# Attention heads paired by kind, scores on two row halves of TensorE, w_in loaded pair by pair

## The chip, the cores and the metric

The kernel runs on one core of a Trainium2 chip. A core has five engines with instruction queues of their own: TensorE (PE in the profile, its weight loads PEld), VectorE (DVE), ScalarE (ACT), GpSimd (POOL) and SyncE (SP). Each works its queue off in order and waits for the others by semaphores. Transfers from and to HBM are issued from the queues of SyncE, ScalarE and GpSimd, and run on 16 DMA engines[...]. The metric is the time of the program on the device in microseconds; the median of three runs is given with the lowest and the highest.

## The reference

Attention over 4 batches, 8 heads, 768 positions of 64 elements, followed by a feed-forward layer with a parametric ReLU. Heads 0, 2 and 6 ("retrieval") see every earlier position. The other five ("streaming") see the first 4 positions (sinks) and the last 64.

```python
scores = q @ k.T / sqrt(64)
scores = where(mask, scores, -1e9)            # causal, or causal and (sink or within 64)
a = exp(scores - max); a = a / sum(a)
x = (a @ v)  ->  [3072 tokens, 8 heads * 64 = 512]
h = x @ w_in                                  # 512 x 2048
g = maximum(h, 0) + alpha * minimum(h, 0)     # alpha: one factor for each of 2048
out = g @ w_out                               # 2048 x 512
```

Inputs and output are fp32; the kernel multiplies in bf16 and sums in fp32.

## The kernel before, in words

**Segments.** Work is cut into 16 segments of one head pair each: segment n is batch n // 4, pair n % 4. A pair's two heads are hh = 0 and 1, and lie side by side on partitions 0 to 63 and 64 to 127 of q and of the attention result. `PAIRS` (line 98) is (0, 1), (2, 3), (6, 7), (4, 5): three pairs of a retrieval and a streaming head, one of two streaming heads.

**Items.** Each step has a short name, and the list `ORDER` (lines 14 to 70) says in what order the steps are recorded. Every engine gets its instructions in that order. No scheduler moves anything: what stands earlier in the list stands earlier in its engine's queue. The names, n for the segment, hh for the head, m for a part:

- `Lqn`, `Lkn`, `Lvn`: loads of q, k, v from SyncE's queue (`load_q` at line 196, `load_k` at 202, `load_rows` at 217). `Cq`, `Ck`, `Cv` cast to bf16, for batch 0 and part of batch 1 on GpSimd, later on VectorE.
- `Tq`, `Tk` transpose on TensorE (line 348) in batches 0 and 1, `tq`, `tk` copy the result to `qT` and `kT`. In batches 2 and 3 transposing DMAs (`Dq`, `Dk`) do it.
- `Sn.hh.m`: scores, `S_retr` (line 405) or `S_stream` (lines 438 and 444); `sn.hh.m`: exponential on ScalarE (lines 415, 463, 469); `mn.hh.m`: multiplication by the mask on VectorE. Batch 0 adds the mask on TensorE instead (lines 408 and 447). `kT` holds each head's k on its own 64 partitions with zeros on the others, so that a score matmul runs over all 128 rows and takes one head's q from the pair's.
- `An.hh`: A·V for the head (line 501), with a column of ones in `vb` for the sums; `an.hh`: reciprocal and multiplication on VectorE (lines 510 and 511).
- `Xn`, `xn`: the pair's result is transposed into `xT`, on TensorE (line 523) or by DMA.
- `Pt.f`: first layer of token block t, for 128 or 256 of the 2048 columns (P1, line 543); `pt.f`: ReLU of the negated on ScalarE (line 548); `gt.f`: combination on VectorE (line 555). In token block 0 the first six `P0.f` are cut into three parts by pair, so that they can start before the last pair is there.
- `Ot.s.u`: a quarter of the second layer for 128 tokens (P2, line 563); `ot.s`: copy on ScalarE and store (lines 569 and 573). The very last 128 tokens are computed in two column halves, `L0`, `L1` with `l0`, `l1` (line 579).
- `wi0` to `wi3`, `wo0` to `wo3`: loads of w_in and w_out from GpSimd's queue, which cast to bf16 on the way (lines 646 and 649). `gate` is one small GpSimd memset on a q buffer ahead of them. `La` loads alpha from ScalarE's queue, `Al` transposes it on TensorE (line 593).

**Tiles of queries.** Keys are cut into tiles of 128 rows. Which query tile starts where is held in `Tiles`: `FAR` (batches 0 and 1) steps by 124, `NEAR` (batches 2 and 3) by 112, since a streaming head's key tile also holds the four sinks. Both have seven query tiles; a retrieval head paired with a streaming head uses the same ones.

**Banks.** PSUM has eight banks. `take` picks, among those that an item may use, the bank given back longest ago; `give` hands it back. Scores use banks 0 and 1 (`SC`), the feed-forward layer 2 to 5 (`FF`), A·V and transpositions 6 and 7 (`MISC`); batch 0 and the ends have lists of their own (`SC2`, `LEAD`, `TAIL`).

Of the kernel before, what the change touches and what calls it, by code (L numbers as in the profile page):

```python
# [9 lines left out]
ALU = mybir.AluOpType  # L10
# [4 lines left out]
Lq0.0 sz0 id Lk0 Lq0.1 zero kz1 kz0 Lq1 nms vz3 kz2 nmr Ck0.0 warm Cq0.0 Tq0.0 Ck0.1 m13.0.2 qz0 Cq0.1 Lk1 sz2 Tk0.0  # L15
kz3 Lq2 Cq1 vz0 tk0.0 Tk0.1 tq0.0 S0.0.0 S0.0.2 Ck1.1 s0.0.0 Lv0 Tq0.1 S0.0.1 Ck1.0 Lk2 Tq1 s0.0.2 qz sz1 s0.0.1 tk0.1
gate tq0.1 Cq2 Cv0 Tk1 Ck2.0 tq1 Ck2.1 S0.1.1 vz1 tk1.0 s0.1.1 tk1.1 Lv1 so vo S0.1.0 s0.1.0 ro Lk3 Lq3 Tq2 S1.0.0 Cv1
s1.0.0 S1.0.2 idf A0.1 A0.0 s1.0.2 tq2 a0.1 S1.0.1 vz2 a0.0 wi0 S1.1.0 s1.0.1 Lv2 Tk2 A1.0 Ck3.1 S1.1.1 tk2.0 s1.1.0
S2.0.0 Cq3 s1.1.1 Ck3.0 s2.0.0 X0 a1.0 S2.0.1 kfz2 A1.1 Cv2 tk2.1 Tq3 a1.1 x0 Tk3 s2.0.1 tq3 tk3.0 S2.1.1 s2.1.1
S2.0.2 X1 S2.1.0 s2.0.2 A2.0 S3.0.1 s2.1.0 tk3.1 x1 S3.0.0 A2.1 s3.0.1 kfz0 La S3.1.0 a2.0 Lv3 P0.2.0 s3.0.0 wi1  # L20
S3.1.1 a2.1 X2 s3.1.1 s3.1.0 Cv3 A3.0 P0.0.0 x2 P0.2.1 a3.0 P0.0.1 Lk4 A3.1 P0.1.0 Al m4.0.2 P0.3.0 a3.1 Ck4.0 P0.1.1
P0.3.1 one X3 wi2 P0.5.0 x3 Ck4.1 P0.4.0 ms wi3 Lk5 P0.0.2 Ck5.0 P0.4.1 Lq4 P0.5.1 p0.0 P0.5.2 p0.5 P0.2.2 kfz1 P0.4.2
al Lv4 Cq4 p0.4 P0.3.2 g0.0 Ck5.1 g0.5 p0.3 p0.2 wo0 Lq5 Tk4 g0.4 g0.3 Tq4 tq4 P0.1.2 P0.6 P0.7 m14.0.2 p0.1 Tk5 P0.10
p0.7 g0.2 P1.0 tk4.0 Lk6 g0.1 Lq7 g0.7 p0.10 g0.10 Lq6 S4.0.1 wo2 p0.6 p1.0 S4.0.0 P0.11 g0.6 P0.9 mr g1.0 s4.0.1
S4.0.3 s4.0.0 S4.0.5 p0.11 s4.0.3 P0.12 wo1 p0.9 s4.0.5 g0.11 P0.14 tk4.1 nz0 p0.12 S4.0.4 g0.9 wo3 s4.0.4 S4.0.2
P0.13 Cq5 p0.14 tk5.0 S4.1.2 g0.12 Lk7 P1.4 P0.15 g0.14 m4.0.3 s4.0.2 tk5.1 S4.1.0 p0.13 s4.1.2 m4.0.4 Tq5 nr g0.13
m4.0.1 S4.1.1 P1.2 P0.8 p0.15 Lk8 Ck6.0 tq5 s4.1.0 s4.1.1 p1.4 S5.0.2 p0.8 s5.0.2 Lv5 Ck6.1 m4.0.0 m4.0.5 S5.0.0
s5.0.0 g0.15 Cv4 Cv5 g1.4 g0.8 A4.0 P1.12 Tk6 P1.8 p1.2 a4.0 S5.0.1 O0.1.0 Cq6 g1.2 p1.8 s5.0.1 m4.1.1 m5.0.0 Tq6
S5.0.4 tq6 s5.0.4 tk6.0 P1.6 p1.6 Lv6 Lq8 m4.1.0 S5.0.3 m4.1.2 g1.8 A4.1 O0.0.0 p1.12 S5.1.2 s5.0.3 O0.0.1 O0.0.2
tk6.1 s5.1.2 S5.0.5 S6.0.1 Cq7 Lq9 Ck7.1 g1.6 P1.10 s5.0.5 g1.12 a4.1 S5.1.0 m5.0.5 m5.0.1 p1.10 s5.1.0 Lv7 X4 Ck8 Tq7  # L30
m5.1.0 s6.0.1 O0.1.1 S5.1.1 Lk10 S6.0.4 m5.0.4 s6.0.4 O0.1.2 tq7 kfz3 nz1 Ck7.0 s5.1.1 g1.10 m5.0.3 O0.2.0 x4 S6.1.0
m5.1.1 Tk7 s6.1.0 A5.0 m5.1.2 m6.0.1 S6.0.2 tk7.0 tk7.1 O0.0.3 s6.0.2 m6.1.0 S7.0.0 S7.0.2 O0.1.3 s7.0.0 s7.0.2 S6.0.3
Cv6 Cq8 A5.1 O0.3.0 S6.1.1 o0.0 m6.0.4 m7.0.0 a5.1 P1.14 s6.0.3 m6.0.3 Dq8 Dk8.0 m7.0.2 S6.1.2 Cq9 s6.1.1 a5.0 p1.14
S6.0.0 s6.1.2 s6.0.0 O0.3.1 O0.3.2 S6.0.5 S7.0.1 m6.1.1 s6.0.5 X5 O0.2.1 m6.0.0 m6.1.2 g1.14 Lk9 m6.0.5 Dk8.1 S7.1.2
s7.0.1 S7.1.1 x5 s7.1.2 A6.1 O0.3.3 m7.0.1 m7.1.2 o0.3 S7.1.0 a6.1 s7.1.0 s7.1.1 Cv7 ns A6.0 O0.2.2 S8.0.0 m7.1.0
S8.0.4 Lq10 s8.0.0 O0.2.3 a6.0 O1.0.0 m7.1.1 A7.0 o0.1 S8.0.1 A7.1 Ck9 s8.0.4 S8.0.2 a7.0 s8.0.1 o0.2 Dq9 Dk9.0 Lv8
O1.0.1 S8.0.5 a7.1 Ck10 X6 s8.0.2 Dk9.1 Lq12 s8.0.5 S8.0.3 X7 x6 O1.0.2 S8.1.1 x7 s8.1.1 P2.0 O1.0.3 p2.0 S8.1.0
s8.1.0 P2.4 s8.0.3 p2.4 Cq10 S9.0.0 g2.0 P2.8 Dk10.1 near g2.4 o1.0 p2.8 P2.7 S9.0.1 m8.0.4 s9.0.1 m8.1.1 P2.5 m12.0.2
s9.0.0 P2.2 m8.0.0 Dq10 S8.1.2 p2.5 g2.8 Cv8 S9.0.2 s9.0.2 Lk12 s8.1.2 p2.7 O1.1.0 g2.5 O1.1.1 Dk10.0 g2.7 S9.0.4
m8.1.0 p2.2 g2.2 m8.1.2 P2.1 P2.13 S9.0.5 p2.1 s9.0.4 P2.9 p2.9 S10.1.0 g2.1 P2.6 m9.0.1 s9.0.5 p2.13 p2.6 Cq12 Lk11  # L40
Lq11 O1.1.2 s10.1.0 g2.9 m9.0.0 P2.3 S9.1.0 g2.13 p2.3 m8.0.5 P2.11 s9.1.0 g2.6 m8.0.3 A8.1 p2.11 m8.0.1 g2.11 A8.0
S10.0.5 P2.12 Lv9 g2.3 S9.1.1 s10.0.5 m9.0.4 Ck11 S10.1.2 P3.4 s10.1.2 S10.0.1 O1.1.3 P2.10 p3.4 a8.1 s10.0.1 s9.1.1
g3.4 S10.1.1 o1.1 s10.1.1 P3.10 Cq11 a8.0 S9.0.3 p2.12 P3.2 Lv10 S10.0.0 m9.1.0 p2.10 p3.10 Lq14 s9.0.3 g2.12 g2.10
g3.10 s10.0.0 P3.14 S9.1.2 Ck12 Cv9 s9.1.2 P2.15 S10.0.4 Dk11.1 p2.15 Dq11 O2.1.0 m9.1.1 m9.1.2 g2.15 m10.1.1 A9.1
m9.0.5 S10.0.3 O2.1.1 P2.14 s10.0.3 m9.0.3 p3.2 A9.0 g3.2 S11.1.2 p2.14 Dk11.0 m10.1.2 g2.14 O2.0.0 s10.0.4 p3.14 P3.6
m10.0.1 s11.1.2 g3.14 Dq12 S10.0.2 m10.0.5 S11.0.0 P3.0 s11.0.0 S11.0.1 Cq14 p3.0 s10.0.2 O2.0.1 a9.1 s11.0.1 m10.0.4
m10.1.0 Lv11 O2.0.2 Cv10 A10.1 O2.1.2 S11.1.0 S11.0.2 O2.0.3 Dk12.0 p3.6 s11.0.2 g3.0 a9.0 O2.1.3 Dk12.1 m11.0.1
S11.1.1 m10.0.0 m11.0.0 Lv12 Lk13 s11.1.0 m10.0.3 o2.1 o2.0 Cv11 A10.0 S12.0.5 s11.1.1 m11.0.2 X9 O2.2.0 m11.1.2 a10.1
S12.1.0 O2.3.0 s12.1.0 P3.8 Lk14 g3.6 a10.0 p3.8 A11.0 O2.2.1 m11.1.0 Lq13 O2.2.2 m11.1.1 S12.0.0 s12.0.5 A11.1
S12.0.3 g3.8 Ck13 X8 s12.0.3 P3.12 s12.0.0 S12.1.1 O2.2.3 m12.1.0 S12.0.4 Ck14 O3.0.0 s12.0.4 Dk13.0 s12.1.1 m12.0.0  # L50
S12.0.2 Cq13 m12.1.1 a11.0 s12.0.2 O3.0.1 O2.3.1 O2.3.2 S12.0.1 O3.0.2 p3.12 a11.1 Cv12 X10 m6.0.2 o2.2 Dq13 X11
m12.0.4 x11 O2.3.3 P4.5 s12.0.1 Dk13.1 Lq15 S13.0.0 s13.0.0 S12.1.2 g3.12 o2.3 m13.0.0 s12.1.2 O3.0.3 p4.5 Dk14.1 Dq14
S13.1.2 o3.0 P4.1 m12.0.5 g4.5 Cq15 S13.0.1 p4.1 P4.6 g4.1 P4.7 s13.1.2 S13.1.0 m12.0.3 m13.1.2 m12.0.1 p4.7 P4.0
s13.0.1 P4.10 p4.6 Lk15 A12.0 p4.0 g4.7 S13.0.3 Dk14.0 Lv13 s13.1.0 P4.4 S13.0.2 g4.0 m13.1.0 m12.1.2 p4.10 A12.1 P4.3
g4.10 s13.0.2 s13.0.3 g4.6 Ck15 Lv14 p4.4 g4.4 P4.8 p4.3 S13.1.1 S13.0.4 P4.2 g4.3 s13.1.1 a12.0 p4.8 s13.0.4 p4.2
P4.11 S14.1.0 g4.8 m13.0.1 g4.2 s14.1.0 m5.0.2 m13.0.4 p4.11 P4.15 S13.0.5 p4.15 g4.11 m13.1.1 S14.0.5 Dq15 Cv13
O3.1.0 s14.0.5 P4.12 s13.0.5 S14.0.1 S14.1.1 Cv14 m14.1.0 p4.12 g4.15 a12.1 Dk15.1 P4.14 s14.0.1 A13.1 Dk15.0 S14.0.3
g4.12 m13.0.3 P4.9 s14.1.1 S14.0.4 O3.1.1 m10.0.2 p4.14 s14.0.3 m13.0.5 s14.0.4 S15.1.0 S15.0.2 O3.1.2 s15.1.0 S14.0.0
P5.2 m14.1.1 Lv15 s14.0.0 g4.14 s15.0.2 a13.1 S14.1.2 X12 O3.1.3 A13.0 S15.0.0 o3.1 m14.0.1 P4.13 P5.10 p4.9 m14.0.4
g4.9 p5.2 m15.1.0 m14.0.5 s15.0.0 S14.0.2 s14.1.2 g5.2 S15.0.1 P5.0 P5.6 m14.1.2 p4.13 p5.10 s15.0.1 p5.0 m14.0.0  # L60
S15.1.2 g4.13 g5.10 O4.0.0 g5.0 A14.1 s15.1.2 O4.2.0 m15.0.1 S15.1.1 s14.0.2 O4.2.1 m15.0.2 m14.0.3 a14.1 p5.6 Cv15
m15.1.2 g5.6 O4.0.1 a13.0 A14.0 P5.8 P5.12 s15.1.1 m15.0.0 a14.0 A15.0 m15.1.1 O4.0.2 A15.1 a15.0 p5.8 O4.2.2 O4.0.3
a15.1 X15 g5.8 X14 O4.1.0 O4.1.1 O4.2.3 p5.12 O4.1.2 g5.12 O4.1.3 P5.4 X13 x15 P7.0 o4.1 O4.3.0 o4.0 p5.4 O4.3.1 P6.8
O4.3.2 P5.14 p6.8 g5.4 O4.3.3 P6.6 P6.12 p6.12 g6.12 O5.0.0 o4.2 O5.0.1 P7.6 p5.14 P6.13 g5.14 o4.3 P6.3 g6.8 p6.3
P7.2 g6.3 p7.0 O5.0.2 O5.1.0 p7.2 g7.0 P6.14 g7.2 p6.6 p6.13 g6.13 P6.7 P6.5 p6.5 O5.1.1 g6.6 P6.10 p6.14 P6.0 g6.14
g6.5 P6.2 O5.1.2 p6.7 p6.2 O5.1.3 g6.7 P6.1 O5.0.3 p6.10 g6.10 p7.6 P7.10 g7.6 P6.4 o5.0 o5.1 g6.2 P6.11 p6.0 P7.14
P6.9 p6.4 g6.0 p6.1 g6.4 p7.10 g7.10 P7.4 p7.4 O7.0.0 g6.1 P6.15 g7.4 P7.8 p6.9 p6.15 g6.9 p6.11 O6.2.0 g6.11 P7.12
O6.2.1 O6.1.0 g6.15 O6.0.0 O6.0.1 O6.2.2 O6.0.2 O6.2.3 p7.8 O7.0.1 O6.1.1 g7.8 o6.2 O6.1.2 O6.0.3 O6.3.0 m9.0.2 O6.1.3
O6.3.1 O6.3.2 m8.0.2 o6.0 p7.12 o6.1 g7.12 p7.14 g7.14 O7.0.2 O6.3.3 o6.3 O7.0.3 o7.0 L1 L0 l1 l0
""".split()  # L70


@with_exitstack
def kernel(
    ctx: ExitStack,
    tc: tile.TileContext,
    q: bass.AP,
    k: bass.AP,
    v: bass.AP,
    is_retrieval: bass.AP,  # L80
    n_sink: bass.AP,
# [10 lines left out]
    n_tok = B * S  # L92
    scale = 1.0 / (D ** 0.5)
    fp32 = DT.float32
    bf16 = DT.bfloat16

    RETR = [1, 0, 1, 0, 0, 0, 1, 0]
    PAIRS = [(0, 1), (2, 3), (6, 7), (4, 5)]
    NSINK = 4
    NT = 7  # L100
    SLOT = 256
    LAY = 8
    XD = (0, 1, 2)
    CROSS = 8
# [16 lines left out]
    def tiles(n):  # L121
        return NEAR if n >= LAY else FAR

# [232 lines left out]
    def put_k(key, n, hh, done=True):  # L356
# [6 lines left out]
        if done:  # L363
            give(held.pop(key))
# [426 lines left out]
```

## Time and profile before

| | |
|---|---|
| Median of 3 runs | 237.03 us (236.91 to 238.66) |
| Profiled execution, in all | 237.75 us |
| Its span | 236.0 us |
| TensorE busy | 226.6 us, 96% of the span |
| VectorE busy | 160.2 us, 68% |
| ScalarE busy | 137.1 us, 58% |
| GpSimd busy | 45.2 us, 19% |
| Matmuls recorded | 1997 (the program has 2026) |
| Read from HBM, written | 27.55 MB, 6.29 MB |

Times in the profile count from the start of the span. A row of a group names line, engine and operation, out and in tensors, and their shape; then its count, busy time and mean duration; then the idle time of the engine before it, with what ended most of it. A matmul's record lasts from its start to the end of its results, so the records of successive matmuls overlap, and the distance between starts is what one costs. The chain of waits is followed back from the last instruction, at each step to what released it, and merges like pieces. A few matmul records are missing. The granted TensorE clock was 1.00 throughout the profile.

### The profile page before, as it was taken

Reading aid. Unit: us, or ns where it says so; the run is one execution under the profiler, and the core shown is the slowest. Engines: PE = TensorE matmul, PEld = TensorE weight load, DVE = VectorE, ACT = ScalarE, POOL = GpSimd, SP = SyncE. Lnnn points to the kernel's source line nnn. Section 1 sums busy time; section 2 is a strip of 40 time slices with the busy share of each in tenths; the row PEclk is TensorE's granted clock in tenths of the full one; section 3 lists DMA queues with packets and bytes.
Section 4 is the critical chain, followed back from the end, with each engine's and each line's share of the span. In section 5 each row is a group of like instructions: output and inputs, shape, how many; then the busy total and the mean of one; then the engine's idle time right before and its main releaser. Section 6 shows DMA issues by size and latency. Waiting matters only on the chain.

```text
span 236.0 us, 5222 instructions
## 1 busy us (share of the span) xinstructions
PE 226.6 (96%) x1997; PEld 143.2 (61%) x2026; DVE 160.2 (68%) x404; ACT 137.1 (58%) x265; POOL 45.2 (19%) x92
## 2 busy tenths in 40 slices
PE   7889899999999999999999999999999999999994
PEld 6679555676666644676666455567755554565453
DVE  5879669997998766788994568967961057563020
ACT  6768349988674676785743567858312253650240
POOL 5775884000311800000010010000001010100000
PEclk9999999999999999999999999999999999999999
DMA  6999999998959999998989999961032020010123
GB/s 196 305 247 243 259 247 250 228 204 182 215 89 207 206 240 221 223 156 184 187 174 186 178 244 141 178 95 44 3 68 87 4 89 1 22 71 0 44 102 123
DMA packets 90529, 36.25 MB, mean 154 GB/s; under 512 B 77688, under 2 KB 88712, under 8 KB 90504
## 3 DMA queue, kind: packets, MB, share of 16 engines
q1 hardware_dynamic: 84520, 26.66, 58.4%
q0 software_dynamic: 5664, 8.91, 17.3%
q8 instruction: 16, 0.26, 0.5%
q10 hardware_dynamic: 320, 0.34, 0.4%
q14 instruction: 9, 0.07, 0.1%
HBM read 27.55 MB, written 6.29 MB: 143 GB/s over the span
## 4 chain that ended last, share of the span: by engine, by line
PE 81%; DMA 5%; SPq 4%; DVE 4%; issue 2%; ACT 2%; POOL 0%; POOLq 0%; DVEq 0%; ACTq 0%
PE P L543 33%; PE P L563 31%; PE P L501 6%; PE P L405 4%; DMA vf<-in_v_dram 3%; DMA alpha_r<-in_moe_alpha_dram 2%; PE P L438 2%; PE P L579 1%; SPq L232 1%; DVE g L555 1%; SPq L210 1%; SPq L234 1%; PE P L642 1%; PE P L523 1%; PE P L444 1%
## 5 line engine op out<-in xcount | busy, mean ns | idle before, releaser
L555 DVE SCALAR_TENSOR_TENSOR g<-neg,oma,P 128x256 bf16<-128x256 f32 (+1 forms) x128 | 72.7, 609 | 46.7 <-ACT neg L548 45.5
L543 PE MATMUL P<-xT,w_in_b 128*128 128x256 bf16 (+1 forms) x499 | 92.5, 324 | 0.7
L563 PE MATMUL P<-w_out_b,g 128*128 128x512 bf16 x352 | 86.4, 379 | 0.8
L548 ACT ACTIVATE neg<-P 128x512 f32<-128x512 f32 x96 | 55.0, 606 | 33.5 <-PE P L543 30.3
L543 PEld LDWEIGHTS <-w_in_b 128*128 128x128 bf16 x512 | 48.7, 98 | 29.2 <-issue 0.4
L563 PEld LDWEIGHTS <-g 128*128 128x128 bf16 x368 | 34.0, 98 | 33.4
L415 ACT ACTIVATE eR<-P 128x488 bf16<-128x488 f32 (+4 forms) x63 | 38.0, 624 | 19.2 <-PE P L405 16.6
L573 POOL DMA_DIRECT2D out_dram<-ot x18 | 10.3, 573 | 124.2 <-ACT ot L569 116.6
L569 ACT COPY ot<-P 128x512 f32<-128x512 f32 x23 | 13.2, 589 | 25.1 <-PE P L563 22.7
L405 PE MATMUL P<-qT,kT 128*128 128x280 bf16 (+16 forms) x132 | 24.3, 272 | 0.2
L511 DVE TENSOR_TENSOR xn<-P,rcp 128x448 bf16<-128x448 f32 x32 | 20.0, 624 | 1.1
L463 ACT ACTIVATE eS<-P 128x352 bf16<-128x352 f32 x30 | 14.1, 475 | 8.1 <-PE P L438 8.1
L469 ACT ACTIVATE eS<-P 128x384 bf16<-128x384 f32 (+1 forms) x25 | 13.5, 558 | 5.2 <-PE P L444 2.2
L405 PEld LDWEIGHTS <-kT 128*128 128x128 bf16 x132 | 11.2, 97 | 7.1 <-DVE kT L368 0.2
L501 PE MATMUL P<-vb,eR 128*128 128x65 bf16 x324 | 11.9, 193 | 0.4 <-ACT eR L415 0.3
L501 PEld LDWEIGHTS <-eR 128*128 128x128 bf16 x324 | 11.1, 97 | 1.9 <-ACT eR L415 0.4
L501 PEld LDWEIGHTS <-eS 128*128 128x128 bf16 x260 | 10.3, 97 | 3.0 <-DVE vb L278 0.5
L501 PE MATMUL P<-vb,eS 128*128 128x65 bf16 x260 | 11.1, 193 | 0.3 <-DVE vb L278 0.3
L444 PE MATMUL P<-qT,kT 128*128 128x192 bf16 (+2 forms) x70 | 10.4, 234 | 0.2 <-ACT eR L415 0.2
L478 DVE TENSOR_TENSOR eS<-eS,ms_near 128x352 bf16<-128x352 bf16 x30 | 9.7, 334 | 1.3 <-ACT eS L463 1.3
L333 POOL CAST vb<-vf 128x896 bf16<-128x896 f32 x6 | 5.6, 933 | 25.9 <-DMA vf<-in_v_dram 24.9
L372 DVE COPY kT<-P 64x744 bf16<-64x744 bf16 x9 | 8.4, 933 | 1.6 <-ACT kT L368 1.4
(98 smaller groups left out, 189.7 us busy)
## 6 DMA issues: line engine op xcount, KB each, us to landing
qf<-in_q_dram SPq DMA_DIRECT2D x15, 384.0 KB
out_dram<-ot POOLq DMA_DIRECT2D x18, 256.0 KB, 3.8
vf<-in_v_dram SPq DMA_DIRECT2D x22, 192.0 KB
kf<-in_k_dram SPq DMA_DIRECT2D x21, 192.0 KB
w_in_b<-in_moe_w_in_dram POOLq DMA_DIRECT2D x4, 512.0 KB, 9.6
w_out_b<-in_moe_w_out_dram POOLq DMA_DIRECT2D x4, 512.0 KB, 18.4
kf<-in_k_dram SPq DMA_DIRECT2D x9, 196.0 KB
vf<-in_v_dram SPq DMA_DIRECT2D x9, 196.0 KB
```

What stands on the lines that cost most here:

```text
L405: nc.tensor.matmul(sc[:, x, a - lo:z - lo], kt[:, 128 * j:128 * (j + 1)], qt[:, c:c + z - a], start=True, stop=not masked)
L415: nc.scalar.activation(ebuf[n, hh][:, lo:hi].rearrange("p (x c) -> p x c", x=len(parts)), P[:, got[0]:got[0] + len(parts), 0:(hi - lo) // ...
L444: nc.tensor.matmul(sc[:, x, o:o + w], kt[:, 128 * j:128 * (j + 1)], qt[:, 124 * j:124 * j + w], start=True, stop=n >= 4)
L463: nc.scalar.activation(slots, sc[:, 0:352].rearrange("p (s c) -> p s c", c=176), AF.Exp, scale=scale)
L469: nc.scalar.activation(slots, sc.rearrange("p x (s c) -> p x s c", c=192), AF.Exp, scale=scale)
L501: nc.tensor.matmul(pav[:, i, :], e[:, o:o + 128], vv[:, j, hh, 0:D + 1], start=(m == 0), stop=(m == len(terms) - 1))
L511: nc.vector.tensor_tensor(xn[n][:, :, 64 * hh:64 * hh + 64], pav[:, :, 0:D], rcp.to_broadcast([128, NT, D]), op=ALU.mult)
L543: nc.tensor.matmul(psg[:, w * i:w * (i + 1)], w_in_b[:, a, 128 * fb:128 * (fb + 1)], xT[:, c, o:o + w], start=(c == 0), stop=(c == 3))
L548: nc.scalar.activation(neg[t, f], bank(held["P", t, f][0]), AF.Relu, scale=-1.0)
L555: nc.vector.scalar_tensor_tensor(g_buf[t % 2][:, fb, 0:w], neg[t, f][:, c], oma[:, fb:fb + 1], bank(got[0])[:, c], op0=ALU.mult, op1=ALU.add)
L563: nc.tensor.matmul(bank(held["O", t, s][0]), g_buf[t % 2][:, f, 128 * s:128 * (s + 1)], w_out_b[:, f, :], start=(f == 0), stop=(f == 15))
L569: nc.scalar.copy(ot, bank(got[0]))
```

## The change

- `PAIRS` becomes (0, 2), (1, 3), (4, 6), (5, 7): one pair of two retrieval heads, one of a streaming and a retrieval head, two of streaming heads. For the first pair there is `FULL`: six query tiles of 128, no sinks, in all batches. `A`, `a` and `X` take the number of tiles from it. A pair's heads are no longer neighbours in memory, so q of batches 2 and 3 takes one load for each head, and `w_in` is stored by pair in the order of `PAIRS`.
- w_in comes in 16 loads (`wi0` to `wi15`), each 512 columns of one pair's 128 rows; `gate` is gone.
- Scores of batches 1 to 3 are gathered (`one_score`) while the list holds only further scores and steps of other engines that `beside_burst` names, and are emitted (`emit_burst`) before anything else. If each of the two heads has at least `SPLIT` = 576 columns in the burst, matmuls of the two go out in alternation, each over its own 64 rows; else as before over 128.
- In batches 1 to 3 every item may take any of the eight banks (`ANY`).
- The last 128 tokens are computed in three column cuts of 256, 128 and 128. `near` is three items, one for each streaming buffer. `put_k` hands its bank back after whichever head comes second.
- `ORDER` is new throughout. Among its changes: `La` is fifth in the list instead of standing after the scores of segment 3, and `Lk2` and `Lk3` stand ahead of `Lv0`.

```diff
-    PAIRS = [(0, 1), (2, 3), (6, 7), (4, 5)]
+    PAIRS = [(0, 2), (1, 3), (4, 6), (5, 7)]
...
+    FULL = Tiles([128 * i for i in range(6)], [128] * 6)
+
+    def full(n):
+        return all(RETR[h] for h in PAIRS[n % 4])
 
     def tiles(n):
-        return NEAR if n >= LAY else FAR
+        return FULL if full(n) else NEAR if n >= LAY else FAR
...
-    SC = [(0,), (1,)]
+    ANY = [(b,) for b in (0, 1, 2, 3, 4, 5, 6, 7)]
     SC2 = [(0, 1), (2, 3)]
-    FF = [(2,), (3,), (4,), (5,)]
...
+    SPLIT = 576
+    burst = []
+
+    def one_score(n, hh, m, to, keys, queries, stop=True):
+        if n < 4:
+            nc.tensor.matmul(to, keys, queries, start=True, stop=stop)
+        else:
+            burst.append((n, hh, m, to, keys, queries))
+
+    def emit_burst():
+
+        halves = [[x for x in burst if x[1] == hh] for hh in range(2)]
+        columns = [sum(x[5].shape[1] for x in half) for half in halves]
+        if min(columns) < SPLIT:
+            for x in burst:
+                nc.tensor.matmul(*x[3:6], start=True, stop=True)
+        else:
+            at = [0, 0]
+            while halves[0] or halves[1]:
+                hh = min((h for h in range(2) if halves[h]), key=lambda h: at[h])
+                to, keys, queries = halves[hh].pop(0)[3:6]
+                own = slice(D * hh, D * hh + D)
+                nc.tensor.matmul(to, keys[own], queries[own], start=True, stop=True)
+                at[hh] += max(65, queries.shape[1]) + 5.5
+        burst.clear()
+
+    def beside_burst(name):
+
+        if name[0] == "S" and int(name[1:].split(".")[0]) >= 4:
+            return True
+        if name[0] == "s" and name[1].isdigit():
+            return tuple(int(x) for x in name[1:].split(".")) not in [x[0:3] for x in burst]
+        return name[0] in "Cpgmaxo" and name[1].isdigit() or name[0] == "L" and name[1] in "qkv"
...
-        for i in range(NT):
+        nt = len(QS)
+        held["A", n, hh] = got = take(*(MISC if n < 4 else ANY))
...
-    def P2_half(t, s, half):
-        held["L", half] = got = take(*TAIL)
-        c = slice(256 * half, 256 * half + 256)
+    CUTS = [0, 256, 384, 512]
+    def P2_cut(t, s, x):
+        held["L", x] = got = take(*TAIL)
+        lo, hi = CUTS[x:x + 2]
...
-    def load_w_in(lo, hi):
-        nc.gpsimd.dma_start(w_in_b[:, :, lo:hi], moe_w_in[:, lo:hi].rearrange("(a p) f -> p a f", p=128))
+    def load_w_in(n):
+        c, lo = n % 4, n // 4 * 512
+        first = heads(c)[0]
+        nc.gpsimd.dma_start(w_in_b[:, c, lo:lo + 512],
+                            dram(moe_w_in, D * first * d_ff + lo,
+                                 [[D * (heads(c)[1] - first) * d_ff, 2], [d_ff, D], [1, 512]]))
...
     for name in ORDER:
+        if not beside_burst(name):
+            emit_burst()
         I[name]()
+    emit_burst()
     return nc
```

## The prediction

> **What bounds the kernel now.** I read the page's shares first, then the busy time by stage, the chain of waits for the spacing of the matmuls, what TensorE waited for, and the order of time around the only long wait. The shares:
>
> ```profile
> PE 226.6 (96%) x1997; PEld 143.2 (61%) x2026; DVE 160.2 (68%) x404; ACT 137.1 (58%) x265; POOL 45.2 (19%) x92
> ```
>
> TensorE is busy for 96% of the span, but a matmul's record overlaps the next, so this is not yet a proof. Busy time by stage (PE, weight loads, DVE, ACT, POOL, clock, DMA share, GB/s):
>
> ```profile
> 0.00:25.00 25.00, 22.03 (x335) 19.23 (x337) 19.90 (x51) 18.60 (x24) 16.12 (x36) 1.00 1.03 254
> 25.00:31.00 6.00, 4.61 (x57) 2.94 (x57) 2.38 (x7) 1.61 (x3) 5.94 (x13) 1.00 1.23 225
> 31.00:64.00 33.00, 32.38 (x285) 21.00 (x287) 30.73 (x76) 27.97 (x54) 8.38 (x12) 1.00 1.12 221
> 64.00:112.00 48.00, 47.63 (x445) 29.50 (x449) 38.12 (x100) 31.47 (x66) 8.15 (x21) 1.00 1.08 191
> 112.00:176.00 64.00, 63.47 (x583) 39.63 (x590) 49.04 (x136) 37.33 (x82) 3.34 (x6) 1.00 0.78 139
> ```
>
> The proof is the spacing. In the chain of waits (start, length, what) the matmuls stand back to back:
>
> ```profile
> 171.05 0.40 PE P L501 x13
> ...
> 174.43 0.39 PE P L523 x7
> ...
> 179.13 1.75 PE P L543 x16
> 180.88 1.73 PE P L563 x8
> ```
>
> 512 columns take 1.73/8 = 216 ns, 256 take 109, 128 take 56, 65 take 30: 0.417 ns a column and 2.3 ns each, with no less than some 65 columns. Charging each of the 2026 matmuls so gives P1 83.1, P2 82.8, scores 24.8, A·V 17.2, transposes 9.9, masks 3.6, warm-up 1.5: 222.9 us. TensorE runs from 1.44 us to about 232.8, so 8.5 us are stalls: 1.5 in the warm-up at line 642 (26 matmuls in 2.96 us), about 5 before 31 us, 2 from 31 to 64, nothing later. After 64 us only fewer or cheaper matmuls help. The longest wait is before that:
>
> ```profile
> 27.85 0.59 PE L543 MATMUL P<-xT,w_in_b 128*128 128x512 bf16 x2
> 29.69 0.20 PE L593 MATMUL P<-ident_f,alpha_r 16*128 16x16 f32 x1 [1.25 <-DMA alpha_r<-in_moe_alpha_dram]
> 29.83 1.04 PE L543 MATMUL P<-xT,w_in_b 128*128 128x512 bf16 x3
> 30.70 0.55 PE L523 MATMUL P<-ident,xn 128*128 128x128 bf16 x7
> ```
>
> The alpha load was issued at 24.17 us (`La`) and TensorE stood still for it. Behind it X3, the transposition of the last pair of batch 0, ran at 30.70. GpSimd shows what fed that pair, with the price of a w_in load and of an output store of 128 rows:
>
> ```profile
> 24.26 0.93 POOL L333 CAST vb<-vf 128x896 bf16<-128x896 f32 x1 [3.05 <-DMA vf<-in_v_dram]
> ```
>
> ```profile
> L646 POOL DMA_DIRECT2D w_in_b<-in_moe_w_in_dram x4 | 3.1, 786 | 0.0
> ```
>
> ```profile
> L573 POOL DMA_DIRECT2D out_dram<-ot x18 | 10.3, 573 | 124.2 <-ACT ot L569 116.6
> ```
>
> [...]
>
> **Part 1, pairs 0-2, 1-3, 4-6, 5-7.** Heads 0 and 2 become a pair of 128-query tiles: six tiles, not seven. A·V per such head has 21 matmuls, not 27: 8 heads x 6 = 48 x 30 ns = 1.4 us. Two X transpositions fewer: 0.1. Score columns of retrieval heads fall from 33,936 to 32,816: 0.5 us, and 20 fewer pieces under 65 columns save some 0.2. Sum 2.2 us. The A·V is on TensorE, the bound. VectorE's smaller masks and the 384-column normalisation (624 ns at 448) save below 1 us of an engine with room. Loading q of batches 2 and 3 takes two issues instead of one, 8 more on SyncE at about 0.5 us, ahead of later k and v loads; 139 GB/s and a DMA share of 0.78 from 112 us on cover it.
>
> **Part 2, score bursts.** Scores of batches 1 to 3 are held back until something other than a listed item comes, and where both heads have 576 columns or more they go out in alternation, each on its own 64 rows. The instruction order of the changed kernel has 13 such bursts, 151 matmuls, 29,459 columns; the longer half of each adds to 15,948. By the spacing above they cost 12.7 us in series and 6.9 as the longer halves: 5.8 us less[...]. Against it stand 26 changes of mode. The trace has one near it: the alpha transposition on 16 rows starts at 29.69, the next full matmul at 29.83, 0.14 us where 0.03 is due, so 0.11. Low end: 0.03, one short matmul[...]. High end: a 65-column matmul is recorded at 193 ns and its spacing is 30[...]: 0.26. I take 0.11, the measured one: 26 x 0.11 = 2.9 us; ends 0.8 and 6.8.
>
> **Part 3, banks.** All eight banks serve everything in batches 1 to 3. A burst takes up to seven of them, and emptying seven takes ScalarE about 7 x 579 ns (exponentials of 488 columns) = 4.1 us. TensorE needs a fresh bank every 0.87 us of P1, though a P2 group lasts 3.5 us on one. Cover: relu and exponentials alternate in the new order. DVE was 93% busy from 31 to 64 us with 2 us of stalls, and has 38.12 of 48 and 49.04 of 64 later; the same work in some 3% less time still fits. I take 0.5 us of new stalls; ends 0 and 4.
>
> **Part 4, the front.** `La` moves right behind ScalarE's first load, so the 1.4 us gap at 28 us goes. Next late is X3: v of the last pair arrived at 24.26; its cast (0.93) and sink copies (0.63) end near 25.9, the second A3 ran at 27.45 to 28.0, its normalisation (198 + 624 ns) ends near 28.8. With 0.5 us of margin X3 moves from 30.7 to 29.3. The new TensorE order has 21.6 us of matmuls ahead of X3, where the old has 22.6; that 1.0 of the savings lies where the loads set the pace, and is not gained. The w_in loads: 16 issues on GpSimd at about 573 ns are 9.2 us, where 4 took 3.1. Nine, not two, stand before the last v cast: 9 x 0.57 - 2 x 0.83 = +3.5 us on that queue, against 8.9 us idle up to 25 us, 3.05 of them just before that cast. The bytes ahead of it are 2.4 MB for 2.1, 1 us at 254 GB/s. I take both as hidden; ends 0 and +1.5 us. `gate` leaves, one memset of 0.1 us on GpSimd.
>
> **Part 5, the end.** The last copy takes 128 columns instead of 256 (373 ns): 0.1 us less. `near` in three pieces costs VectorE 0.3 us in its slack.
>
> **The sum.** The profiled execution took 237.75 us, 236.0 of span and 1.7 around it, 0.7 over the median of 237.03. From 237.75: -2.2 (pairs) -1.4 (alpha) +1.0 (work ahead of X3, not gained) +0.5 (banks) -0.1 (end) = 235.55; -5.8 +2.9 (bursts) = 232.65. Less 0.7, on the scale of the medians: **231.9 us**.
>
> **The rivals.** *A, the mode changes cost more than the pairing gives*: the halves run one behind the other, or nearly[...]. Without the bursts the median is 234.8; with no overlap it is 234.8 + 26 s, 241.6 at s = 0.26, and over +1% from s = 0.18. [...] Against: the measured 0.11[...]. This is the slower side. *B, banks take the place*: each burst leaves TensorE waiting 0.3 us for ScalarE, 13 x 0.3 = 3.9: 235.8, no change that can be told. For it: 93% DVE in one stage; against: ACT is at 58%. *C, changes nearly free* (0.03) and the front a further 1 us shorter: 231.9 - 2.1 - 1 = 228.8. For it: 5 us of stalls before 31 us.
>
> **The chances.** Forecast 0.62 (229.5 to 234.6), A 0.12, B 0.12, C 0.14. A measurement of this kernel tells about 1% from no change. Faster by over 1% (below 234.7): 0.62 + 0.14 + a little of B = 0.78; within: 0.11; slower: 0.11. The range is 227.0 to 237.5: it takes in C with a margin and B, and leaves out A's dear end.
>
> **What would show it.** TensorE's records of the burst line on 64 rows, in pairs that start a few ns apart (right), or one full length apart (A). The gap between the last full matmul and a burst's first, and at its end: 0.1 us each. A·V x276 on eR for x324. No wait of line 593's successor for alpha; X3 near 29. Waits of TensorE for ScalarE or VectorE behind bursts above 1 us in all would be B. The forecast is wrong above all if the price of a mode change is.

## The result, and the profile after

The changed kernel takes **247.52 us** (median of 4 runs, 246.31 to 249.27) against 237.24 us for the kernel before, measured beside it: a ratio of 1.043, 95% interval 1.035 to 1.051. It is slower; the forecast was 231.9 us with a range that ended at 237.5. Here and below the medians take in all executions, and the ratios leave out those more than 1.5% above the fastest of the same kernel. The profiled execution took 249.27 us with a span of 247.6.

The page of the changed kernel: shares of the engines, granted clock by fortieths of the span, and the chain of waits by engine.

```profile
PE 228.1 (92%) x1992; PEld 138.7 (56%) x1992; DVE 157.3 (64%) x409; ACT 136.6 (55%) x266; POOL 54.6 (22%) x103
...
PEclk9999858799999999999999999999999999999999
...
PE 74%; DMA 17%; DVE 3%; ACT 2%; issue 1%; SPq 1%; POOL 0%; POOLq 0%; ACTq 0%
```

The chain of the kernel before:

```profile
PE 81%; DMA 5%; SPq 4%; DVE 4%; issue 2%; ACT 2%; POOL 0%; POOLq 0%; DVEq 0%; ACTq 0%
```

There DMA held 5%, and the clock stayed at 9 throughout. Here DMA holds 17%, and the clock dips in four slices between 25 and 50 us. Busy time by stage says where (columns as in the prediction):

```profile
0.00:25.00 25.00, 20.96 (x283) 17.83 (x284) 18.26 (x50) 18.61 (x24) 19.64 (x39) 1.00 0.97 211
25.00:31.00 6.00, 2.09 (x47) 1.69 (x46) 1.61 (x4) 1.62 (x3) 3.60 (x8) 0.86 1.19 235
31.00:42.00 11.00, 8.54 (x57) 4.67 (x57) 4.11 (x7) 0.22 (x1) 6.82 (x10) 0.61 1.24 241
42.00:64.00 22.00, 16.25 (x108) 10.00 (x109) 12.71 (x23) 14.06 (x26) 11.42 (x24) 0.92 1.29 183
64.00:112.00 48.00, 48.00 (x469) 28.23 (x467) 41.00 (x127) 36.06 (x77) 5.77 (x12) 1.00 0.85 171
112.00:176.00 64.00, 64.00 (x537) 37.37 (x536) 49.39 (x128) 40.06 (x89) 4.06 (x7) 1.00 0.90 170
```

From 64 us on TensorE is busy all the time, as before. The loss lies between 25 and 64 us: 2.09 us of work in 6, then a clock of 0.61, then 16.25 in 22. The order of time on TensorE names the cause (start, length, what, and in brackets the idle time ahead of it with what ended it):

```profile
26.98 0.38 PE L597 MATMUL P<-xT,w_in_b 128*128 128x512 bf16 x1
31.31 0.61 PE L597 MATMUL P<-xT,w_in_b 128*128 128x512 bf16 x1 [3.95 <-DMA w_in_b<-in_moe_w_in_dram]
34.53 1.03 PE L597 MATMUL P<-xT,w_in_b 128*128 128x512 bf16 x2 [1.90 <-DMA w_in_b<-in_moe_w_in_dram]
...
39.38 0.64 PE L578 MATMUL P<-ident,xn 128*128 128x128 bf16 x7
...
46.90 1.89 PE L597 MATMUL P<-xT,w_in_b 128*128 128x512 bf16 x4 [5.15 <-DMA w_in_b<-in_moe_w_in_dram]
49.83 4.06 PE L597 MATMUL P<-xT,w_in_b 128*128 128x512 bf16 x22
```

Three waits for w_in, 11.0 us together, stand where the kernel before had none. X3 runs at 39.38 instead of 30.70. A matmul of 512 columns is recorded at 0.61 us behind the first wait and at 0.38 ahead of it: TensorE's clock had been halved. The trace's clock record has it at half for 10.2 us from 29.3 and for 3.4 us from 46.4. The stretches between the changes of the clock in the front are 7, 3, 2 and 1 times 3.41 us, so it is read in windows of that length. In the one ahead of the first fall TensorE's records cover 43% of the time; the windows of all profiles are counted behind e5. TensorE worked for some 9.2 of the 13.7 us at half clock, so that about 4.6 us of the loss are this at most, by estimate. Work that was slowed ahead of the wait at 46.90 need not have cost anything, since that wait ended with a landing.

What the loads did, in the changed kernel (group, software queue with packets and MB, time from issue to landing):

```profile
L706 POOL DMA_DIRECT2D w_in_b<-in_moe_w_in_dram x16 | 12.7, 806 | 6.3 <-DMA w_in_b<-in_moe_w_in_dram 6.1
...
q0 software_dynamic: 20192, 8.97, 20.0%
...
DMA to landing us min/median/max: 11.4/15.1/20.2
```

and in the kernel before:

```profile
q0 software_dynamic: 5664, 8.91, 17.3%
...
DMA to landing us min/median/max: 7.6/9.6/12.1
```

A load of a quarter of the bytes takes 15.1 us to land where the large one took 9.6, and the queue handled 14,528 packets more for 0.06 MB more. GpSimd itself, which also casts v, stood idle for 6.1 us ahead of these loads until earlier ones of w_in had landed.

### The profile page after: what moved, and what is told of

Same layout as the page of the kernel before. It is cut to its first block, busy times and chain, and to the rows that moved or that the text cites. A ratio compares the mean times of both kernels' runs of the same rounds, so it can differ in the third digit from the quotient of the medians.

```text
span 247.6 us, 5211 instructions
## 1 busy us (share of the span) xinstructions
PE 228.1 (92%) x1992; PEld 138.7 (56%) x1992; DVE 157.3 (64%) x409; ACT 136.6 (55%) x266; POOL 54.6 (22%) x103
## 3 DMA queue, kind: packets, MB, share of 16 engines
q0 software_dynamic: 20192, 8.97, 20.0%
## 4 chain that ended last, share of the span: by engine, by line
PE 74%; DMA 17%; DVE 3%; ACT 2%; issue 1%; SPq 1%; POOL 0%; POOLq 0%; ACTq 0%
PE P L617 32%; PE P L597 29%; DMA w_in_b<-in_moe_w_in_dram 13%; PE P L553 5%; PE P L427 3%; DMA vf<-in_v_dram 2%; DMA kf<-in_k_dram 2%; DVE g L609 2%; PE P L420 2%; PE P L636 1%; PE P L578 1%; ACT neg L602 1%; PE P L362 1%; DVE kT L385 0%; DVE kT L389 0%
## 5 line engine op out<-in xcount | busy, mean ns | idle before, releaser
L597 PE MATMUL P<-xT,w_in_b 128*128 128x512 bf16 (+1 forms) x512 | 93.6, 332 | 11.9 <-DMA w_in_b<-in_moe_w_in_dram 11.0
L466 ACT ACTIVATE eR<-P 128x448 bf16<-128x448 f32 (+6 forms) x63 | 37.0, 626 | 15.5 <-PE P L427 11.7
L564 DVE TENSOR_TENSOR xn<-P,rcp 128x448 bf16<-128x448 f32 (+1 forms) x32 | 19.4, 607 | 1.1
L706 POOL DMA_DIRECT2D w_in_b<-in_moe_w_in_dram x16 | 12.7, 806 | 6.3 <-DMA w_in_b<-in_moe_w_in_dram 6.1
L563 DVE RECIPROCAL rcp<-P 128x7 f32<-128x7 f32 (+1 forms) x32 | 6.3, 197 | 12.1 <-PE P L553 11.8
L410 PE MATMUL P<-qT,kT 128*128 128x192 bf16 (+13 forms) x68 | 11.1, 251 | 0.6 <-DVE qT L367 0.5
L476 DVE TENSOR_TENSOR eR<-eR,mr_near 128x128 bf16<-128x128 bf16 (+5 forms) x36 | 7.3, 224 | 4.5 <-ACT eR L466 4.5
L553 PE MATMUL P<-vb,eR 128*128 128x65 bf16 x276 | 10.1, 192 | 0.0
L553 PEld LDWEIGHTS <-eR 128*128 128x128 bf16 x276 | 9.4, 97 | 0.8
L427 PE MATMUL P<-qT,kT 64*128 64x176 bf16 (+15 forms) x151 | 9.3, 246 | 0.0
## 6 DMA issues: line engine op xcount, KB each, us to landing
w_in_b<-in_moe_w_in_dram POOLq DMA_DIRECT2D x16, 128.0 KB, 15.1
```

Of the source, the lines that this page charges most:

```text
L427: nc.tensor.matmul(to, keys[own], queries[own], start=True, stop=True)
L466: nc.scalar.activation(ebuf[n, hh][:, lo:hi].rearrange("p (x c) -> p x c", x=len(parts)), P[:, got[0]:got[0] + len(parts), 0:(hi - lo) // ...
L553: nc.tensor.matmul(pav[:, i, :], e[:, o:o + 128], vv[:, j, hh, 0:D + 1], start=(m == 0), stop=(m == len(terms) - 1))
L564: nc.vector.tensor_tensor(xn[n][:, 0:nt, D * hh:D * hh + D], pav[:, :, 0:D], rcp.to_broadcast([128, nt, D]), op=ALU.mult)
L597: nc.tensor.matmul(psg[:, w * i:w * (i + 1)], w_in_b[:, c, 128 * fb:128 * (fb + 1)], xT[:, c, o:o + w], start=(c == 0), stop=(c == 3))
L706: nc.gpsimd.dma_start(w_in_b[:, c, lo:lo + 512], dram(moe_w_in, D * first * d_ff + lo, [[D * (heads(c)[1] - first) * d_ff, 2], [d_ff, D], ...
```

## Experiments

The median of the kernel before lay between 237.5 and 238.1 us beside the various runs; a ratio is always to the runs on the same chip. Theory T of the expectations is that the pattern of the source, two groups of 64 rows, makes each load slow.

**e1, each load cut into its two heads.**

```diff
-        nc.gpsimd.dma_start(w_in_b[:, c, lo:lo + 512], dram(..., [[D * (heads(c)[1] - first) * d_ff, 2], [d_ff, D], [1, 512]]))
+        for hh, h in enumerate(heads(c)):
+            nc.gpsimd.dma_start(w_in_b[D * hh:D * hh + D, c, lo:lo + 512], moe_w_in[D * h:D * h + D, lo:lo + 512])
```

> The changed kernel with each of the 16 w_in loads issued as two loads of 64 rows, one for each head (32 issues, same places). Theory T[...]: the loads land in under 10 us, the waits of TensorE for w_in (11.0 us) fall below 2 us, the half clock after them goes, and the time falls from 247.5 to 231 to 235 us. Rival R1 (the number of loads and their fixed cost): twice as many loads, 250 us or more. Rival R2 (w_in crowds out the loads of q, k and v because it is issued earlier): about 245.

240.02 us, 1.008 (1.004 to 1.012). Twice as many issues, 32 at a median of 557 ns, and 7.5 us of the loss are gone: the loads land in 5.6 us, and no wait for w_in is left.

```profile
DMA to landing us min/median/max: 4.2/5.6/6.1
```

So neither the number of issues, nor their time on GpSimd (17.8 us in all, for 12.7), nor the bytes in all made the loss. The time stays above the 231 to 235 us of theory T; TensorE now waits 3.2 us for the casts of v, and the clock is halved once.

**e2, the same 16 loads from 128 neighbouring rows.**

```diff
-                            dram(moe_w_in, D * first * d_ff + lo, [[D * (heads(c)[1] - first) * d_ff, 2], [d_ff, D], [1, 512]])
+                            moe_w_in[128 * c:128 * c + 128, lo:lo + 512]
```

> The changed kernel with its 16 w_in loads taken from 128 neighbouring rows each, so that source and target both have 128 as slowest dimension; the rows then belong to other heads than the pair's, and the output is not the reference's. Number, size, order and places of the loads are those of the change. T: 230 to 234 us. R1: 247, unchanged. R2: about 245.

236.03 us, 0.987 (0.985 to 0.990), and 0.993 by the medians of all executions. The landing falls to 6.9 us at the same number, size and place of the loads:

```profile
DMA to landing us min/median/max: 5.6/6.9/8.7
```

What TensorE waits for now is the casts of v:

```profile
PE P L553 <- POOL vb L347: 4.6, 2, 3.4
```

**e3 and e4, the kernel before with 16 loads: of neighbouring rows, and of two groups of 64.**

```diff
-        nc.gpsimd.dma_start(w_in_b[:, :, lo:hi], moe_w_in[:, lo:hi].rearrange("(a p) f -> p a f", p=128))
+        for a in range(4):
+            nc.gpsimd.dma_start(w_in_b[:, a, lo:hi], moe_w_in[128 * a:128 * a + 128, lo:hi])               # e3
+            nc.gpsimd.dma_start(w_in_b[:, a, lo:hi], dram(..., [[2 * D * d_ff, 2], [d_ff, D], [1, hi - lo]]))   # e4
```

> The kernel before with each of its four w_in loads cut into four of 128 neighbouring rows by 512 columns (16 loads, nothing else). T: 237 to 239 us, no more than 12 further issues on GpSimd of 0.6 to 0.8 us. R1: 243 or more.

> As the one with 16 loads in the kernel before, but each takes two groups of 64 rows that are 128 rows apart, the pattern of the changed kernel; the rows are then not those that the tile should hold, and the output is not the reference's. T: loads of 11 to 20 us, TensorE waits for w_in, 243 to 255 us. R1: as with 16 plain loads.

e3 takes 238.71 us, 1.002 (0.999 to 1.005): 16 loads for 4 cost nothing that can be told. e4 takes 254.70 us, 1.067 (1.059 to 1.074): the pattern alone costs the kernel before 16 to 17 us. Software queue and landing of e3:

```profile
q0 software_dynamic: 5856, 8.92, 17.4%
...
DMA to landing us min/median/max: 5.1/7.6/9.5
```

and of e4, with what TensorE waited for most (us in all, times, longest):

```profile
q0 software_dynamic: 20192, 8.97, 19.3%
...
DMA to landing us min/median/max: 9.0/15.3/19.3
...
PE P L543 <- DMA w_in_b<-in_moe_w_in_dram: 10.9, 5, 3.0
```

Between these two only the source pattern differs, at equal number and bytes. That the pattern is the cause was thus measured. How it acts was not shown. The queue of e4 handled 20,192 - 5,856 = 14,336 packets more, 896 for each of the 16 loads, all of them of 4 bytes. No view shows the share of each DMA engine, but the trace has every packet. In the first 1.5 us of its first load of w_in the changed kernel starts 22 data packets of 1,024 bytes and never has more than 2 in flight; e4 starts 28, at most 3 in flight, e5 (next) 80 and at most 14, e3 96 and at most 17. So the slow loads had at most 2 or 3 packets in flight there, the others 14 or 17; on how many engines they ran was not measured.

**e5, the two dimensions in the other order.** A load takes one head's 64 rows of two neighbouring pairs. Number, bytes and places in the queue are those of the changed kernel, as is the place of every weight; the slowest dimension is 64.

```diff
-        c, lo = n % 4, n // 4 * 512
-        nc.gpsimd.dma_start(w_in_b[:, c, lo:lo + 512], dram(..., [[D * (heads(c)[1] - first) * d_ff, 2], [d_ff, D], [1, 512]]))
+        hh, c, lo = n % 2, n % 4 // 2 * 2, n // 4 * 512
+        nc.gpsimd.dma_start(w_in_b[D * hh:D * hh + D, c:c + 2, lo:lo + 512],
+                            dram(moe_w_in, D * heads(c)[hh] * d_ff + lo, [[d_ff, D], [D * d_ff, 2], [1, 512]]))
```

> The changed kernel with each of its 16 w_in loads turned from one pair's 128 rows into one head's 64 rows of two neighbouring pairs: same number, bytes and places, the right rows in the tile, but 64 as slowest dimension on both sides. Theory T[...]: as with plain neighbouring rows, 234 to 238 us, no wait of TensorE for w_in. If that run had its time from anything else than the pattern: nearer to 247.

> e5's kernel once more, to be compared with the two others on one chip: 236 to 238.5, ratio to the kernel before 0.990, within half a per cent of e5's.

e5 has a median of 238.07 us against 238.13 for the kernel before; e11, the same kernel on another chip, 237.98 against 237.48. The pattern's 9.5 us are gone, but the mended change is no faster than the kernel before. The ratios, 0.990 (0.987 to 0.994) and 0.994 (0.991 to 0.997), rest on 22 of its 40 executions. In the profile of e5 (landing, TensorE's longest wait, and that wait in order of time):

```profile
DMA to landing us min/median/max: 5.6/7.9/10.2
...
PE P L553 <- POOL vb L347: 4.1, 1, 4.1
...
30.15 1.17 PE L553 MATMUL P<-vb,eS 128*128 128x65 bf16 x13 [4.06 <-POOL vb L347]
```

The 40 executions of the two series show what goes with the clock. In 15 it stayed full (a mean of 0.998 or more), with a median of 235.5 us (234.6 to 239.1); in 25 the mean was 0.984 to 0.997, by estimate from it half clock for some microseconds, with a median of 238.6 (235.8 to 241.8). Of the executions without a profile only the mean clock is known, so the 3 us may hold longer waits too.

What stands ahead of half clock can be counted in the clock records of the 14 profiles. Cut at the changes of the clock into windows of 3.41 us, they hold 932 whole windows at full clock. In 17 of them TensorE's records cover less than 49% of the time, and half clock followed 16 of these; in the other 915 they cover 49.6% or more, and none was followed by half clock. (The exception, 46.9%, lies at 231.6 us in e11. Ends of matmul records are modelled and a few records are missing, so the bound is a rough one.) Some windows from the front:

| Profile | Window from, us | Covered by records | Longest wait in it or across it, us | Clock after |
|---|---|---|---|---|
| changed kernel | 25.90 | 43% | 3.95 | half |
| e1 | 26.47 | 47% | 2.62 | half |
| e11 | 23.43 | 48.9% | 1.56 | half |
| e4 | 27.85 | 49.6% | 2.25 | full |
| e12 | 32.27 | 53% | 2.89 | full |

So in these profiles it is not the length of one wait that tells the cases apart but the idle time in one window, and where the window lies: the wait of 2.89 us in e12 lies across two windows (53% covered) and the clock stayed full, while in e11 half clock followed one of 1.56 with smaller ones (48.9%). By an estimate from the 3.41 us and the 49%, a single wait of under 1.7 us (half a window) is not enough, and one of over 3.5 us fills half of some window wherever it lies.

**e7, e5 without the bursts.**

```diff
-    SPLIT = 576
+    SPLIT = 1 << 30
```

> The changed kernel with the mended loads and SPLIT so large that no burst goes out in halves: all scores run over 128 rows, in the same order. The forecast's terms (pairing 5.8 us, 26 mode changes at 0.10) say 3.2 us slower than with the halves. Rival A (mode changes eat the gain): the same or faster. Rival B (banks): waits behind bursts stay the same.

241.26 us (9 runs), 3.2 above e5, and 1.005 of the kernel before (1.000 to 1.009; 1.013 by the medians of all executions). In the executions at full clock the difference is much the same, 238.95 (3 of them) for 235.6 (8). Without the bursts the mended change is slower than the kernel before.

**e8, the kernel before with the load of alpha early.** In the order, `La` moves from ahead of `S3.1.0` to right behind `Lk0`.

```diff
-... Lq0.0 sz0 id Lk0 Lq0.1 ...  s3.0.1 kfz0 La S3.1.0
+... Lq0.0 sz0 id Lk0 La Lq0.1 ...  s3.0.1 kfz0 S3.1.0
```

> The kernel before with the alpha load alone moved right behind the first k load. The forecast's term says 1.4 us faster, 235.8 against 237.2. Rival: the next late thing takes the place of the wait for alpha, no more than 0.4 us faster.

237.84 us, 0.999 (0.996 to 1.001). The rival of this run came true: the wait for alpha is gone, but X3 goes from 30.70 only to 30.22, and other waits have grown:

```profile
PE P L347 <- POOL qf L277: 0.8, 1, 0.8
PE P L347 <- POOL g L304: 0.6, 1, 0.6
PE P L542 <- DMA w_in_b<-in_moe_w_in_dram: 0.4, 1, 0.4
```

The first of them was 0.6 before, and the last was not there: the matmul behind X3 now waits for w_in.

**e6, e9, e10, e12: the order of the loads in the front of e5.** The last two casts of v stand at 22.45 and 29.17 us in e5, where the kernel before has 19.02 and 24.26. e6 puts SyncE's loads of batch 0 back in the order of the kernel before; e9 moves five w_in loads behind the last v cast; e10 does both; e12 moves three of the five.

```diff
-... Lk1 ... Lk2 ... Lq2 ... Lk3 ... Lv0 ... Lv1        # e5, e9, e12
+... Lk1 Lq2 Lv0 Lk2 Lv1 Lk3 ...                        # e6, e10
-... wi6 Tq3 ... wi2 wi3 wi11 kfz2 ... wi7 X0 ... Cv3 ... wi9     # e5, e6
+... Cv3 wi2 wi3 wi6 wi7 ... wi9 wi11                             # e9, e10
+... wi2 wi3 kfz2 ... Cv3 wi6 wi7 ... wi9 wi11                    # e12
```

> The same with the loads of batch 0 on SyncE's queue in the order of the kernel before (q2, v0, k2, v1, k3 behind k1), and the four small memsets of the v buffers ahead of them. Theory V (what is left of the front is lost because v of the last two pairs of batch 0 is asked for later): the v casts move up by 3 to 6 us, the waits of TensorE for them (4.6 us) fall below 1.5, the time falls to 230 to 234 us. Rival (w_in takes the DMA engines from v whatever the order of issue): no change, 234 to 238.

> As e5 (one head's 64 rows of two neighbouring pairs per load), with the five loads of pairs 2 and 3 that stood ahead of the last v cast (16 x 128 KB in all, five of them here) issued behind it. Theory front (w_in bytes crowd out v of the last pair): 1.3 MB less ahead of it are 5 us at 254 GB/s, so the last v cast starts near 25 us instead of 29.2, the 4.1 us wait of TensorE for it goes, and the time falls by 2 to 4 us, to 234 to 236. Rival (the wait moves): the loads of pairs 2 and 3 are then issued at 25 to 28 us, land 6 to 8 us later, and TensorE waits for w_in at 30 to 35 us instead; the time stays within 1 us of e5's 238.1.

> The same move on e6 (SyncE's loads of batch 0 in the order of the kernel before). Theory front: the v casts come as early as in the kernel before (19 and 24 us), X3 runs near 31 us, and the time is 233 to 235, some 1.5% below the kernel before. Rival (the wait moves): waits for w_in or for casts of q and k take its place, 237 to 239.

> As e5, with the loads of w_in for pairs 2 and 3, columns 0 to 511, left ahead of the last v cast, and only the three for later columns (0.39 of e9's 0.66 MB) moved behind it. Theory front: 0.39 MB less ahead of v of the last pair are 1.5 us at 254 GB/s and the wait of 4.1 us for its cast shrinks by that, while no wait for w_in as e9's 4.9 us comes; with the shorter idle stretch TensorE keeps its full clock in more of the executions, which was worth 3 us in e5 (235.6 at full clock, 238 to 241 otherwise): 235 to 236.5. Rival (the front is bound by all its loads together, whatever their order): 237.5 to 240, with another wait in that place.

e6: 238.53 us, 1.003 (1.000 to 1.005). e9: 242.52, 1.020 (1.014 to 1.026). e10: 238.75, 1.005 (1.003 to 1.008). e12: 240.86, 1.010 (1.002 to 1.018). None beats e5, and none comes to the times of the theories. In e9 the wait for the cast of v is as good as gone and X3 runs at 31.18, but (TensorE, order of time):

```profile
27.94 0.22 PE L552 MATMUL P<-vb,eS 128*128 128x65 bf16 x2 [0.40 <-POOL vb L346]
...
31.18 0.55 PE L577 MATMUL P<-ident,xn 128*128 128x128 bf16 x7
36.68 5.44 PE L596 MATMUL P<-xT,w_in_b 128*128 128x512 bf16 x12 [4.94 <-DMA w_in_b<-in_moe_w_in_dram]
```

In e12 both waits are there in part:

```profile
PE P L596 <- DMA w_in_b<-in_moe_w_in_dram: 2.9, 1, 2.9
PE P L552 <- POOL vb L346: 2.0, 2, 1.5
```

In e10 it is a cast of q, for 2.9 us at 11 us, and 2.0 us of w_in. The profile of e6 is its fastest execution (235.95) and shows no long wait; 18 of its 21 had the clock halved, and what they waited for was not recorded. The theory that the late casts of v alone hold the front falls: whatever is brought forward, what it passes comes late. The rival of these runs, that the wait moves, stands, though e6 (by 0.5 us), e9 and e12 came out above its ranges too.

## Why the prediction was wrong

**The step that failed: the w_in loads of Part 4.** "I take both as hidden; ends 0 and +1.5 us" priced 16 issues on GpSimd's queue and the bytes ahead of the last v cast, these at 254 GB/s whatever their pattern. The issues were indeed harmless (e3: 16 loads for 4 at no cost that can be told; e1: 32 at no wait for w_in). What the step left out of the sum is the time from issue to landing: it didn't ask what the pattern of the source does to that. The diff shows the pattern: the outermost dimension of the source is two heads. The loads landed in 15.1 us, and TensorE waited 11.0 us for them. Mended, in e5, the change takes 238.07 us for 247.52, so this term was 9.5 us in place of 0, with the half clock behind its waits (10.3 by the medians of the kernel before beside each); in the kernel before the same pattern cost 16 (e4 for e3).

**What is left, 238.07 for 231.9, lies in the front too**, but for 1.1 us by which the kernel before took longer beside e5 (238.13) than in the table that the forecast starts from. *The alpha term*, -1.4 us, was mis-sized: in the kernel before it measured -0.3 (e8, 237.84 for 238.13), not to be told from nothing, since q and w_in were late next, and I had named only X3's own chain. *X3*, forecast at 29.3, stands at 35.52 in the profile of e5, behind the last cast of v:

```profile
29.17 0.93 POOL L347 CAST vb<-vf 128x896 bf16<-128x896 f32 x1 [4.85 <-DMA vf<-in_v_dram]
...
35.52 0.55 PE L578 MATMUL P<-ident,xn 128*128 128x128 bf16 x7
```

The prediction took 3.05 us of idle GpSimd ahead of the last v cast as cover for the w_in loads, but that idle time was a wait for v, and v is among what comes later. From 12 to 25 us e5's DMA moved 186 GB/s, at an average load of 1.08 of its engines; the kernel before moved 247 (12 to 18 us) and 267 (18 to 25) at 1.09 and 1.17. Why the engines moved less at much the same load was not tried. *The half clock* was in no case of the prediction; executions at full clock took 235.5 where the median of all is 238.0. So of the remaining 5.0 us, 1.1 are alpha, 2.5 go with the clock, and some 1.4 are left for the late casts by difference. This is an estimate: the three were not measured apart, and they overlap.

**Part 1, the pairs: not contradicted, not measured alone.** A·V of the retrieval heads has the 276 matmuls forecast. That a short piece costs as much as some 65 columns is in the profile before: from the start of a matmul of 16 to 45 columns to the next start it is 27.5 to 28.5 ns (medians), and 29 for 65 columns. Without the bursts (e7) everything else together is about 3 us slower than the kernel before (241.26 for 238.13), so that the 2.2 us of the pairs, if they were there, were more than used up, by what the traces show in the front.

**Part 2, the bursts: right.** The bursts have their 151 matmuls on 64 rows, and no group of them waited. The profile of the changed kernel:

```profile
L553 PE MATMUL P<-vb,eR 128*128 128x65 bf16 x276 | 10.1, 192 | 0.0
L427 PE MATMUL P<-qT,kT 64*128 64x176 bf16 (+15 forms) x151 | 9.3, 246 | 0.0
```

That the halves would overlap was my assumption, since the profile before has no matmuls on two row halves. By the starts of the matmuls they do: the first two of each burst start 3 to 5 ns apart. The gap at each change of mode, beyond the usual spacing, is 0.095 us going in and 0.092 coming out (medians of 13), where 0.11 was taken: 26 changes are 2.4 us, not 2.9. From their first starts to the next matmul on full rows the 13 bursts take 8.4 us, with the gaps going in 9.6; 6.9 + 2.9 = 9.8 was forecast, and 12.7 is what the spacing gives in series. The net of 2.9 us forecast is thus 3.1 by the trace, and measured 3.2 (e7 against e5). The dear end of a change, 0.26 us, was an estimate from the profile before: 193 ns that a 65-column matmul is recorded, less its spacing of 30, and 98 of a weight load. That a change costs these was not shown.

**Part 3, banks:** 0.5 us of new stalls were taken; from 64 to 212 us the profile of the changed kernel lists no wait of TensorE for ScalarE or VectorE at all, and none is seen there beyond the changes of mode. **Part 5** is too small to be told.

**The rivals.** The sign of A came true, its mechanism did not: the mode changes are a little cheaper than forecast. B was not seen. C's mode changes of 0.03 us were not seen either (0.09), and its shorter front is the opposite of what came. The prediction's closing sentence, that it would be wrong above all by the price of a mode change, looked at the part that was new and not at the one that carried a rewritten transfer.

## What to carry to other kernels

Read a transfer's access pattern as part of its price: don't leave a short dimension (two heads) as the slowest, but put it further in, as e5 does at equal bytes and issues. Measured here are a slowest dimension of 2 (15.1 us to landing, changed kernel), 64 (7.9, e5) and 128 (6.9, e2); other sizes were not. An idle stretch in the front counts as cover only when what ends it doesn't come later by the same change. Waits of TensorE can cost their length and then a halved clock: the changed kernel's first wait for w_in took 3.95 us, and within it the clock fell to half for 10.2 us. What tells the cases apart in these profiles is the idle time within a window of 3.41 us, so that several short waits close together can do it too, as in e11, where the longest was 1.56 us.

## What was not expected of the hardware

- A load with two groups of 64 rows landed in 15.1 us in the kernel after and 15.3 in the kernel before, against 6.9 to 7.9 for loads of equal bytes whose slowest dimension is 128 or 64, and brought 896 packets of 4 bytes more to the queue.
- Its issue on GpSimd is dearer too: 792 ns against 551 (medians of e4 and e3).
- TensorE's clock fell to half behind 16 of the 17 windows of 3.41 us that its records covered by less than 49%, and behind none of 915 others. One such window held no wait over 1.56 us (e11).
- The same instructions in the same order took 234.6 to 241.8 us over 40 executions, some at full clock and some not. The kernel before, whose profile has no wait of TensorE over 1.3 us behind the warm-up, kept its full clock in 48 of the 52 executions beside e5, e5 in 8 of 20.
- A change between full and half rows cost TensorE 0.095 us going in and 0.092 coming out (medians of 13, changed kernel).
